# A planner that gives VectorE and GpSimd their shared way to SBUF in turn, and a weight's sign written as a byte by ScalarE

## The chip, the cores and the metric

The kernel runs on one core of a Trainium2 chip. The core has TensorE (PE in the profile, its weight loads PEld), VectorE (DVE), ScalarE (ACT), GpSimd (POOL), and SyncE (SP), which issues the DMAs here. The metric is the device time of one execution in microseconds; the time before is the median of three runs.

## What is computed

Causal attention for 4 batches of 12 heads (448 rows of 64), then a mixing by the real part of a two-dimensional Fourier transform, a layer norm and a feed-forward of 768 to 3072 to 768:

```python
def _moe_ref(x, w_ch1, w_ch2):
    X = np.fft.fft(np.fft.fft(x, axis=1), axis=2)
    u = x + np.real(X).astype(np.float32)
    mu = np.mean(u, axis=-1, keepdims=True)
    var = np.mean((u - mu) ** 2, axis=-1, keepdims=True)
    un = (u - mu) / np.sqrt(var + 1e-06)
    return (u + np.maximum(un @ w_ch1, 0.0) @ w_ch2).astype(np.float32)

def reference(q, k, v, w_ch1, w_ch2):
    x = attention(q, k, v)          # causal softmax, heads side by side: (4, 448, 768)
    return _moe_ref(x, w_ch1, w_ch2)
```

The two weight matrices arrive as 64-bit floating point numbers. They lie in HBM as pairs of 32-bit words, and the kernel itself makes float32 of them.

## The kernel before

**Stages.** Attention runs over 24 pairs of heads (`attend`), six to a batch. After each batch its Fourier transform and norm follow (`fold`, `dft`), mixed among the next pairs. The feed-forward runs over two groups of two batches, and in each over 12 chunks of 256 hidden columns: `f1` makes the hidden values (L978, PSUM tile h), `f2` multiplies them with the second weights (L1219 for group 0, L1180 for group 1, PSUM tile o) and VectorE adds the result into acc (L1168). Every float32 product is made of three passes over a high and a low half (names ending in h and l; w1 and w2h, w2l are such halves of weights). Chunks before `C_FAST` are multiplied in eight blocks of nine matmuls, later ones in seven by Strassen's scheme (`fast`), which needs sums of blocks of weights (ws, L824) and of inputs (us, L930) and adds the running sums c (copied by L335, added to by L1051). Group 1 uses sums in `f2` too (L867, L878, L1108, L1118).

**Conversion of weights.** In group 0 each chunk needs four halves of 128x768 numbers, two of each matrix, 48 in all. Function `weights` (L733 to L780) takes a half w, whose last axis is the low and the high word: ScalarE writes the magnitude of the high word into w32 (L742) and three low bits, taken from one byte, into the low word (L746). VectorE joins the sign bit with these bits (L752), limits and scales the magnitude (L758), and joins the magnitude, shifted by three bits, with the rest (L762). ScalarE then rounds to the high half (L775, or L335 through `copy`), and the low half is the difference (L779 on GpSimd, or L811 on VectorE or GpSimd). The results are kept in HBM (wf, wp), and group 1 reloads them.

**Order.** Every operation is a unit of the class `Plan`, with a cost, a priority, and the tiles it reads and writes. `order()` takes, over and over, the unit that can start first (then by priority) on a list of engines; a unit that may run on several engines goes to the one where start, a bias and SLOW times its cost are least. Each engine then runs its units in that order, and waits by semaphores for data alone. VectorE and GpSimd share a way to SBUF: for units of GpSimd, and those of VectorE that touch no PSUM tile (`side`), `takes` stretches the costs while both run, to a rate of `BOTH`: 0.42 for VectorE, 0.72 for GpSimd. The tables at the top set how many buffers each tile has (`N_W` for w, `N_W32` for w32, `N_QK`, `N_RAW`, `N_PA`) and when units fall due.

Of the kernel before, what the change touches and what calls it, by code (L numbers as in the profile page):

```python
# [51 lines left out]
W_HIGH = float(np.uint32((1151 << 20) - 1).view(np.float32))  # L52
# [23 lines left out]
class Plan:  # L76
# [11 lines left out]
    def add(self, eng, cost, prio, fn, rd=(), wr=(), phase=None):  # L88
# [8 lines left out]
        self.units.append(dict(  # L97
            n=n, engs=dict(zip(eng, cost)) if many else {eng: cost}, many=many, prio=prio, fn=fn, deps=deps, phase=phase,
            new=sorted({z[:2] for z in wr if z[0] in self.bufs}, key=str)))

    def order(self):
# [87 lines left out]

        while len(seq) < len(units):  # L190
            best = None
            for e, cand in pool.items():
                for n in cand:
                    u = units[n]
                    t = when(n, e)
                    if t is None:
# [16 lines left out]
            u["eng"], cost = e, takes(n, e, t)  # L213
            if e in now and side[e][n]:
                x = "G" if e == "V" else "V"
                o = now[x]
                if o is not None and end[o] > t:
                    late = (min(t + cost, end[o]) - t) * (1 - BOTH[x])
                    end[o] += late
                    free[x] += late  # L220
                    for m in succ[o]:
                        for y in units[m]["engs"]:
                            ready[m][y] = max(ready[m][y], end[o] + self.LAT.get((x, y), 100))
            if e in now:
                now[e] = n if side[e][n] else None
# [39 lines left out]
def tile_kernel(ctx, tc, qk, vv, w1, w2, cc, cd, cs, out):  # L265
    nc = tc.nc if tc else None
    T = {}
# [120 lines left out]
    def attend(i):  # L388
# [50 lines left out]
        for k, rows in enumerate(rows_):  # L439
# [82 lines left out]
        for k, (rd, parts) in enumerate((  # L522
                ([(*pa, 0, 0), (*pa, 0, 384), (*pa, 1, 0)], [(0, 0, S, pa, 0, S)]),
                ([(*pg2, 2, 0)], [(1, 128, 256, pg2, 0, 256)]),
                ([(*pg3, 3, 0), (*pa, 1, 384)],
                 [(2, 256, 128, pg3, 0, 128), (1, 384, 64, pg3, 256, 64), (2, 384, 64, pg3, 384, 64), (3, 384, 64, pa, 896, 64)]))):
            def f(parts=parts):
                for c, q0, w, src, s0, sd in parts:
                    kk = min(128, S - 128 * c)
                    for h in range(2):  # L530
# [52 lines left out]
    def dft(b, p0, dp):  # L583
# [6 lines left out]
        for par in range(2):  # L590
# [47 lines left out]
            for sign in range(2):  # L638
# [84 lines left out]
    def weights(j, nm, half, p0):  # L723
# [670 lines left out]
```

## Time and profile before

| what | value |
|---|---|
| median of the runs | 942.95 us (942.83 to 944.33) |
| profiled execution, span | 942.7 us, 16159 instructions |
| TensorE busy | 903.4 us (96%) |
| VectorE busy | 796.9 us (85%) |
| GpSimd busy | 627.6 us (67%) |
| ScalarE busy | 545.3 us (58%) |
| HBM | 112.89 MB read, 54.74 MB written |

TensorE's matmuls are pipelined, so its busy share says that something is in its pipe, not that it runs at its peak. A VectorE or GpSimd instruction counts as busy while it waits for the shared way, so its mean length against its shortest tells of that waiting.

### The profile page before, as it was taken

To read this page: it belongs to the slowest core of one execution; us is meant where nothing else is said; L and a number is where in the kernel's file an instruction comes from. 1 tells how busy PE (TensorE), PEld (TensorE's weight loads), DVE (VectorE), ACT (ScalarE), POOL (GpSimd) and SP (SyncE) were. 2 spreads that over 40 slices of the span, in tenths; PEclk is the share of its full clock that TensorE was granted. 3 is DMA by queue.
4 is the path that set the end of the run, shared out by engine and by line. 5 is a ranking of instruction groups with operands and counts; after the bars stand their busy time and mean duration, and the time that the engine had idled before them with its cause. 6 is when DMAs were issued, how large, how long until landed. Compare 5 with 4: busy or idle time off the path is not lost.

```text
span 942.7 us, 16159 instructions
## 1 busy us (share of the span) xinstructions
PE 903.4 (96%) x5636; PEld 805.8 (85%) x5636; DVE 796.9 (85%) x1330; ACT 545.3 (58%) x1300; POOL 627.6 (67%) x648
## 2 busy tenths in 40 slices
PE   7999999999799999999999988999999999999998
PEld 4667668777688999988989887998999999999998
DVE  6889999898897887999998999997788676666668
ACT  6999798988644444545454456645454453444442
POOL 4798698884642222443543337799999898887886
PEclk9999999999899999999999999999999999999999
DMA  7624624615569556758777668665123444444403
GB/s 274 220 88 170 183 77 138 164 45 180 149 210 345 171 208 224 245 196 292 277 275 256 214 217 295 210 217 174 48 68 118 129 139 136 141 145 136 149 1 117
DMA packets 67537, 165.84 MB, mean 176 GB/s; under 512 B 18976, under 2 KB 31904, under 8 KB 67360
## 3 DMA queue, kind: packets, MB, share of 16 engines
q1 hardware_dynamic: 67456, 164.82, 52.8%
q8 instruction: 44, 0.72, 0.3%
q14 instruction: 37, 0.30, 0.1%
HBM read 112.89 MB, written 54.74 MB: 178 GB/s over the span
## 4 chain that ended last, share of the span: by engine, by line
PE 60%; DVE 21%; POOL 6%; issue 6%; ACT 6%; DMA 1%; SPq 0%; POOLq 0%; DVEq 0%; ACTq 0%
PE h L978 22%; PE o L1180 16%; PE o L1219 8%; PE x L531 4%; PE pt L505 3%; PE sc L457 3%; DVE acc L1168 3%; DVE w L762 3%; DVE w L752 2%; ACT p L473 2%; DVE w L811 1%; DVE w L758 1%; DVE mn L469 1%; DVE ws L824 1%; DVE hl L1015 1%
## 5 line engine op out<-in xcount | busy, mean ns | idle before, releaser
L1168 DVE TENSOR_TENSOR acc<-o,acc 128x384 f32<-128x384 f32 x444 | 236.8, 552 | 79.9 <-PE o L1180 56.3
L1219 PE MATMUL o<-w2l,hh 128*128 128x384 f32 x336 | 113.6, 338 | 1.4 <-POOL w2l L779 1.3
L1219 PE MATMUL o<-w2h,hh 128*128 128x384 f32 x336 | 113.3, 337 | 1.6 <-DVE acc L1168 1.6
L1219 PE MATMUL o<-w2h,hl 128*128 128x384 f32 x336 | 113.1, 337 | 0.0
L779 POOL TENSOR_TENSOR w2l<-w,w2h 128x768 fp32r<-128x768 f32 x24 | 49.7, 2071 | 78.6 <-ACT w2h L775 71.6
L494 POOL TENSOR_TENSOR p<-p,ri 128x128 f32<-128x128 f32 (+3 forms) x113 | 79.1, 729 | 22.0 <-DVE ri L485 18.1
L811 POOL TENSOR_TENSOR w<-w,w 128x384 fp32r<-128x384 f32 x33 | 39.7, 1203 | 60.1 <-ACT w L335 59.1
L978 PE MATMUL h<-u11h,w 128*128 128x448 f32 x174 | 64.8, 380 | 3.4 <-ACT u11h L335 3.0
L1219 PEld LDWEIGHTS o<-w2l,hh 128*128 128x128 f32 x336 | 63.1, 188 | 4.4 <-POOL w2l L779 2.6
L1219 PEld LDWEIGHTS o<-w2h,hh 128*128 128x128 f32 x336 | 63.2, 188 | 4.2 <-DVE acc L1168 2.3
L978 PE MATMUL h<-u22h,w 128*128 128x448 f32 x174 | 63.2, 371 | 3.2 <-DVE c L1051 3.2
L1180 PE MATMUL o<-w2h,hh 128*128 128x384 f32 x288 | 65.1, 339 | 0.3 <-DVE acc L1168 0.3
L978 PE MATMUL h<-u12h,w 128*128 128x448 f32 x174 | 64.1, 370 | 0.0
L1219 PEld LDWEIGHTS o<-w2h,hl 128*128 128x128 f32 x336 | 63.2, 188 | 0.0
L978 PE MATMUL h<-u21h,w 128*128 128x448 f32 x174 | 63.0, 367 | 0.0
L1180 PE MATMUL o<-w2l,hl 128*128 128x384 f32 x288 | 62.4, 338 | 0.4 <-DVE acc L1168 0.4
L505 PE MATMUL pt<-cst,p 128*128 128x128 f32 (+1 forms) x384 | 56.9, 281 | 2.6 <-ACT p L492 1.9
L505 PEld LDWEIGHTS pt<-cst,p 128*128 128x128 f32 (+1 forms) x384 | 41.4, 139 | 16.8 <-issue 5.7
L335 ACT COPY c<-h 128x448 f32<-128x448 f32 x57 | 30.1, 529 | 44.1 <-PE h L978 40.2
L867 POOL TENSOR_TENSOR w2h<-w,w2h 128x384 fp32r<-128x384 f32 x43 | 45.8, 1065 | 14.6 <-ACT w2h L335 14.6
L473 ACT ACTIVATE p<-sc,mn 128x448 f32<-128x448 f32 (+3 forms) x96 | 50.4, 525 | 7.6 <-DVE mn L469 6.7
L1180 PEld LDWEIGHTS o<-w2h,hh 128*128 128x128 f32 x288 | 52.1, 188 | 2.6 <-DVE acc L1168 0.6
(212 smaller groups left out, 2999.7 us busy)
## 6 DMA issues: line engine op xcount, KB each, us to landing
w<-in_w_dram SPq DMA_DIRECT2D x48, 768.0 KB, 4.9
wp<-w SPq DMA_DIRECT2D x49, 384.0 KB, 3.5
w<-wp SPq DMA_DIRECT2D x49, 384.0 KB, 3.1
wf<-w SPq DMA_DIRECT2D x34, 384.0 KB, 2.9
w<-wf SPq DMA_DIRECT2D x17, 768.0 KB, 4.3
raw<-in_qk_dram SPq DMA_DIRECT2D x23, 480.0 KB, 3.8
us<-und SPq DMA_DIRECT2D x45, 224.0 KB, 4.2
v<-in_vv_dram SPq DMA_DIRECT2D x24, 256.0 KB, 2.9
```

The lines of the kernel that those rows point to most:

```text
L335: nc.scalar.copy(out=out, in_=in_)
L473: nc.scalar.activation(out=T[pb][:, PO[rr]:PO[rr] + n], in_=T[ps][:, c0:c0 + n], func=ACTF.Exp, scale=-1.0, bias=T[mn][:, rr:rr + 1], accu ...
L494: nc.gpsimd.tensor_tensor(out=x, in0=x, in1=z.to_broadcast([128, KE[r]]), op=ALU.mult)
L505: nc.tensor.transpose(T[ps][0:m, 128 * k:128 * k + 128], T[pb][:, PO[r] + 128 * c:PO[r] + 128 * c + m], T["cst", 0][:, 0:128])
L531: nc.tensor.matmul(out=T[xps][64 * h:64 * h + 64, q0:q0 + w], lhsT=T[v][0:kk, c, h * D:(h + 1) * D], rhs=T[src][0:kk, s0 + h * sd:s0 + h * ...
L779: nc.gpsimd.tensor_tensor(out=T[wl], in0=T[w32].bitcast(F32), in1=T[wh], op=ALU.subtract)
L811: (nc.gpsimd if eng == "G" else nc.vector).tensor_tensor(out=T[z][:, 1], in0=src(), in1=T[z][:, 0], op=ALU.subtract)
L867: (nc.gpsimd if eng == "G" else nc.vector).tensor_tensor(out=T[z][:, 384:768], in0=src(), in1=T[z][:, 0:384], op=ALU.subtract)
L978: nc.tensor.matmul(out=T[ps][:, 0:S], lhsT=a[:, t], rhs=x[:, t], start=start and k == 0, stop=stop and k == 8, skip_group_check=True)
L1168: nc.vector.tensor_tensor(out=x, in0=T[ps][:, 0:384], in1=x, op=ALU.add)
L1180: nc.tensor.matmul(out=T[ps][:, 0:384], lhsT=hpart(j, h, a)[:, k * 128:k * 128 + 128], rhs=T[z][:, 384 * b:384 * b + 384], start=start and ...
L1219: nc.tensor.matmul(out=T[ps][:, 0:384], lhsT=T[a][:, m, k * 128:(k + 1) * 128], rhs=w[:, sl], start=(m == 0 and z == 0), stop=(m == 1 and ...
```

## The change

Four things change together.

1. The planner no longer stretches costs. A unit that uses the shared way starts, in the plan, no earlier than 91 ns (VectorE) or 42 ns (GpSimd) before the other engine's last such unit ends (`OVER`). Units given `port=False` (reciprocal, bn_stats, bn_aggr) don't count as users.
2. In `weights`, ScalarE writes the sign as a byte into the top of the low word, by Prelu with a slope of 2^100 for negative numbers, over the three bits' word. VectorE's L752 goes; its last join reads the low word. The scaling moves from VectorE's L758 into ScalarE's L742.
3. Buffers and due times: three w and w32 where there were two, four of each q and k half for three, three raw for two, four c for three, one pa for two; the DMA scratch area of GpSimd shrinks to 1024 bytes. `C_FAST` goes from 5 to 4, `C_MIX` from 7 to 5, and many due times move.
4. Some costs in the tables.

```diff
-N_RAW, N_V, N_QK, N_PT, N_W, N_W32, N_PA = 2, 2, 3, 2, 2, 2, 2
+N_RAW, N_V, N_QK, N_PT, N_W, N_W32, N_PA = 3, 2, 4, 2, 3, 3, 1
-SPLIT_AT, FOLD_AT = -509, 5113
+SPLIT_AT, FOLD_AT = -688, 5956
...
-W_LEAD, F2_LAG = 809, 561
+W_LEAD, F2_LAG = 1065, 508
...
-C_FROM, W_FROM, N_WARM = 0, 8, 11
-N_W1, N_C, N_WS, C_FAST, C_MIX = 7, 3, 3, 5, 7
+C_FROM, W_FROM, N_WARM = 3, 8, 11
+N_W1, N_C, N_WS, C_FAST, C_MIX = 7, 4, 3, 4, 5
...
-BOTH = dict(V=0.42, G=0.72)
-SLOW, BIAS = 1.5, dict(S=-300, V=-100, G=-500)
+OVER = dict(V=91, G=42)
+SLOW, BIAS = 1.843, dict(S=-300, V=-100, G=-427)
...
-        def takes(n, e, t):
-            c = units[n]["engs"][e]
-            o = now.get("G" if e == "V" else "V") if e in now and side[e][n] else None
-            if o is None or end[o] <= t:
-                return c
-            both = end[o] - t
-            return c / BOTH[e] if c <= both * BOTH[e] else c + both * (1 - BOTH[e])
+        held = {"V": 0.0, "G": 0.0}
 
         def when(n, e):
             s = slot(units[n], e)
-            return None if s is None else max(free[e], ready[n][e], s)
+            if s is None:
+                return None
+            t = max(free[e], ready[n][e], s)
+            if e in held and side[e][n]:
+                t = max(t, held["G" if e == "V" else "V"] - OVER[e])
+            return t
...
         def f():
-            nc.scalar.activation(out=T[w32].bitcast(F32), in_=T[w][:, :, 1].bitcast(F32), func=ACTF.Abs)
+            nc.scalar.activation(out=T[w32].bitcast(F32), in_=T[w][:, :, 1].bitcast(F32), func=ACTF.Abs, scale=W_SCALE)
...
         def f():
-            x = T[w][:, :, 1]
+            nc.scalar.activation(
+                out=T[w].bitcast(I8)[:, :, 3], in_=T[w][:, :, 1].bitcast(F32), func=ACTF.Prelu, scale=SIGN_SCALE, alpha=SIGN_ALPHA)
+        add("S", acts(768) + 75, p0 + 1, f, rd=[w, (*w, 1)], wr=[(*w, 2)], phase="W")
+
+        def f():
+            x = T[w32].bitcast(F32)
+            nc.vector.tensor_scalar(out=x, in0=x, scalar1=W_TOP, scalar2=None, op0=ALU.min)
+        add("V", dve(768, 1.92) + 4, p0 + 2, f, rd=[(*w32, 0)], wr=[(*w32, 1)], phase="W")
+
+        def f():
             nc.vector.scalar_tensor_tensor(
-                out=x, in0=x, scalar=0x80000000, in1=T[w][:, :, 0], op0=ALU.bitwise_and, op1=ALU.bitwise_or)
...
-                out=T[w32], in0=T[w32], scalar=3, in1=T[w][:, :, 1], op0=ALU.logical_shift_left, op1=ALU.bitwise_or)
+                out=T[w32], in0=T[w32], scalar=3, in1=T[w][:, :, 0], op0=ALU.logical_shift_left, op1=ALU.bitwise_or)
```

What the change makes of the order is shown at three places. In the kernel after, lines stand some twelve lower: L731, L735 and L740 are ScalarE's passes over a half (L740 the sign), L746 and L750 VectorE's limit and join, L767 the low half on GpSimd, L799 the low halves of w1, L812 the sums ws, L1156 the additions into acc, L918 the sums us, L324 copies and casts, L997 the hidden values, L763 the high half. w_ with a number is a buffer of w1 or w32.

VectorE, one fast chunk late in group 0, before:

```order
L758 TENSOR_SCALAR w_6861<-w_6861 128x768
L1168 TENSOR_TENSOR acc_4497<-o_6864,acc_4497 128x384
L752 SCALAR_TENSOR_TENSOR w<-w 128x768
L1168 TENSOR_TENSOR acc_4497<-o_6875,acc_4497 128x384
L762 SCALAR_TENSOR_TENSOR w_6861<-w_6861,w 128x768
L1168 TENSOR_TENSOR acc_4502<-o_6891,acc_4502 128x384
L824 TENSOR_TENSOR ws<-ws,w_6819 128x384
L811 TENSOR_TENSOR w_6933<-ws,w_6933 128x384
```

and a fast chunk of the kernel after, about as late:

```order
L750 SCALAR_TENSOR_TENSOR w_6766<-w_6766,w 128x768
L812 TENSOR_TENSOR ws<-w_6766 128x384
L1156 TENSOR_TENSOR acc_4532<-o_6804,acc_4532 128x384
L812 TENSOR_TENSOR ws<-ws,w_6696 128x384
L812 TENSOR_TENSOR ws<-w_6696,w_6766 128x384
L1156 TENSOR_TENSOR acc_4534<-o_6820,acc_4534 128x384
L799 TENSOR_TENSOR w_6831<-ws,w_6831 128x384
L799 TENSOR_TENSOR w_6837<-ws,w_6837 128x384
L799 TENSOR_TENSOR w_6847<-ws,w_6847 128x384
L812 TENSOR_TENSOR ws<-w_6696,ws 128x384
```

The join before L762 is gone, and all four sums ws of a chunk stand on VectorE, where one stood.

GpSimd, the same chunks, before:

```order
L811 TENSOR_TENSOR w_6856<-w_6819,w_6856 128x384
L811 TENSOR_TENSOR w_6883<-w_6819,w_6883 128x384
L824 TENSOR_TENSOR ws<-w_6861 128x384
L824 TENSOR_TENSOR ws<-w_6819,w_6861 128x384
L824 TENSOR_TENSOR ws<-w_6819,ws 128x384
L811 TENSOR_TENSOR w_6971<-ws,w_6971 128x384
L779 TENSOR_TENSOR w2l<-w_6963,w2h 128x768
L779 TENSOR_TENSOR w2l<-w_6982,w2h 128x768
```

and after, where between the first row and the last nothing but L767 stands:

```order
L918 TENSOR_TENSOR us<-us 128x448
L767 TENSOR_TENSOR w2l<-w_5514,w2h 128x768
L767 TENSOR_TENSOR w2l<-w_5635,w2h 128x768
L767 TENSOR_TENSOR w2l<-w_5748,w2h 128x768
L767 TENSOR_TENSOR w2l<-w_5977,w2h 128x768
```

Fourteen more rows of L767 follow that differ in the buffer alone. Counted over the whole program, GpSimd has 11 L811 for 58 (2 for 37 ahead of group 1), 6 L824 for 26 (none for 21), 2 L905 for 25, 4 L930 for 11, 31 L867 for 85, 24 L1118 for 38 and 97 L494 for 113; VectorE has most of what these lose; the 16 L494 go to ScalarE.

ScalarE, the conversions of that chunk with the copy of c behind them, before:

```order
L742 ACTIVATE w_6388<-w 128x768
L742 ACTIVATE w_6415<-w 128x768
L746 ACTIVATE w<-w 128x768
L775 CAST w2h<-w_6388 128x768
L1009 ACTIVATE hh<-c 128x448
L335 COPY c<-h 128x448 x2
```

and after:

```order
L731 ACTIVATE w_6562<-w 128x768
L735 ACTIVATE w<-w 128x768
L324 COPY c<-h 128x448
L740 ACTIVATE w<-w 128x768
L997 ACTIVATE hh<-c 128x448
L731 ACTIVATE w_6601<-w 128x768
L763 CAST w2h<-w_6562 128x768
```

Each half has a third pass, L740, among the copies of c and the casts. No load of a function table is added: there is one in the program, before and after.

## Rows read from the trace of the kernel before

**Rows 1.** Busy us by stretch: PE, PEld, DVE, ACT, POOL (count), clock, DMA, GB/s.

```profile
20.00:243.00 223.00, 212.98 (x1940) 156.75 (x1940) 197.32 (x400) 199.42 (x612) 179.10 (x226) 1.00 0.46 141
243.00:300.00 57.00, 52.42 (x306) 48.55 (x307) 51.92 (x76) 27.80 (x51) 28.35 (x27) 0.94 0.73 235
300.00:390.00 90.00, 90.00 (x480) 86.01 (x479) 73.14 (x113) 43.60 (x66) 24.02 (x17) 1.00 0.62 216
390.00:640.00 250.00, 234.91 (x1234) 220.38 (x1232) 236.90 (x335) 128.09 (x222) 130.83 (x95) 1.00 0.71 247
640.00:760.00 120.00, 118.95 (x617) 112.01 (x618) 96.05 (x156) 60.40 (x139) 113.50 (x112) 0.99 0.31 102
```

**Rows 2.** Waits of TensorE in 390 to 640: us in all, times, longest.

```profile
PE h L978 <- ACT c L335: 9.3, 7, 2.8
PE h L978 <- DVE c L1051: 3.2, 3, 1.7
```

**Rows 3.** VectorE's groups in 390 to 640: count, busy us, mean ns, idle before.

```profile
L1168 DVE TENSOR_TENSOR acc<-o,acc 128x384 f32<-128x384 f32 x119 | 61.8, 547 | 5.4 <-PE o L1219 5.3
L762 DVE SCALAR_TENSOR_TENSOR w<-w,w 128x768 uint32<-128x768 uint32 x27 | 32.1, 1189 | 0.0
L752 DVE SCALAR_TENSOR_TENSOR w<-w 128x768 uint32<-128x768 uint32 x26 | 28.9, 1111 | 0.7 <-ACT w L742 0.5 <-ACT w L746 0.2
L1015 DVE SCALAR_TENSOR_TENSOR hl<-c,hh 128x448 fp32r<-128x448 f32 x21 | 19.3, 918 | 2.4 <-ACT hh L1009 2.3
L811 DVE TENSOR_TENSOR w<-ws,w 128x384 fp32r<-128x384 f32 x20 | 16.8, 869 | 0.9 <-ACT w L335 0.9
```

**Rows 4.** Timeline of 420 to 432: start, length (us), instruction.

```profile
421.33 0.96 DVE L752 SCALAR_TENSOR_TENSOR w<-w 128x768 uint32<-128x768 uint32 x1 [0.49 <-ACT w L742]
...
421.77 1.39 POOL L811 TENSOR_TENSOR w<-ws,w 128x384 fp32r<-128x384 f32 x1 [1.92 <-ACT w L335]
...
422.20 1.37 DVE L758 TENSOR_SCALAR w<-w 128x768 f32<-128x768 f32 x1
...
430.07 0.54 DVE L811 TENSOR_TENSOR w<-ws,w 128x384 fp32r<-128x384 f32 x1
...
430.54 0.61 DVE L1015 SCALAR_TENSOR_TENSOR hl<-h,hh 128x448 fp32r<-128x448 f32 x1
...
431.07 0.61 DVE L1015 SCALAR_TENSOR_TENSOR hl<-c,hh 128x448 fp32r<-128x448 f32 x1
```

**Rows 5.** ScalarE's groups in 390 to 640, as rows 3.

```profile
L746 ACT ACTIVATE w<-w 128x768 uint32<-128x768 uint8 x26 | 23.7, 913 | 7.3 <-DMA w<-in_w_dram 7.3
...
L335 ACT COPY c<-h 128x448 f32<-128x448 f32 x25 | 13.1, 527 | 8.0 <-PE h L978 7.3 <-POOL us L1118 0.4
```

**Rows 6.** GpSimd's groups in 390 to 640, as rows 3.

```profile
L779 POOL TENSOR_TENSOR w2l<-w,w2h 128x768 fp32r<-128x768 f32 x15 | 33.1, 2204 | 36.1 <-ACT w2h L775 36.1
L811 POOL TENSOR_TENSOR w<-w,w 128x384 fp32r<-128x384 f32 x15 | 18.7, 1244 | 35.1 <-ACT w L335 35.1
```

**Rows 7.** The chain that ended last, one piece: start, us, what, instructions.

```profile
306.56 3.71 PE h L978 x18
```

**Rows 8.** The same chain where the feed-forward starts.

```profile
242.95 1.59 DVE u11l L905
```

**Rows 9.** Busy time and clock of 240 to 250, as rows 1.

```profile
240.00:250.00 10.00, 5.89 (x16) 5.07 (x17) 9.68 (x10) 6.38 (x13) 9.31 (x8) 0.68 0.42 115
```

**Rows 10.** Groups of three engines in attention, 20 to 243, as rows 3.

```profile
L494 POOL TENSOR_TENSOR p<-p,ri 128x128 f32<-128x128 f32 (+3 forms) x105 | 74.6, 739 | 19.7 <-DVE ri L485 15.8 <-PE sd L457 2.4 <-ACT xt L335 1.1
...
L427 DVE SCALAR_TENSOR_TENSOR ql<-raw,qh 128x512 fp32r<-128x512 f32 x21 | 19.4, 925 | 0.7 <-ACT qh L421 0.7
...
L337 DVE COPY pa<-pt 128x128 f32<-128x128 f32 (+2 forms) x14 | 5.3, 381 | 6.6 <-ACT pa L335 5.5 <-PE pt L505 1.0
```

**Rows 11.** VectorE's timeline in the first pair, as rows 4.

```profile
11.40 0.69 DVE L427 SCALAR_TENSOR_TENSOR ql<-raw,qh 128x512 fp32r<-128x512 f32 x1
```

More of the change, by code (lines that the diff above doesn't have):

```diff
@@ L14 @@
 U8 = mybir.dt.uint8
+I8 = mybir.dt.int8
 ACTF = mybir.ActivationFunctionType
@@ L39 @@
 AFTER = dict(E1=("A1",), E2=("A1", "A2"), L=("Q",))
-C_FROM, W_FROM, N_WARM = 0, 8, 11
-N_W1, N_C, N_WS, C_FAST, C_MIX = 7, 3, 3, 5, 7
-MIX_LEAD, FILL_LEAD = -94, 417
-LATER = dict(S=-1500, V=-248, G=-847)
+C_FROM, W_FROM, N_WARM = 3, 8, 11
+N_W1, N_C, N_WS, C_FAST, C_MIX = 7, 4, 3, 4, 5
+MIX_LEAD, FILL_LEAD = 270, 472
+LATER = dict(S=-1401, V=-399, G=-847)
 F0 = 1e6
 AGAIN = dict(S=-1500, V=-100, G=-1000)
-NORM_AT, TR_AT = 1675, 1894
+NORM_AT, TR_AT = 1675, 1763
 N_UB, N_US = 3, 5
-BOTH = dict(V=0.42, G=0.72)
-SLOW, BIAS = 1.5, dict(S=-300, V=-100, G=-500)
+OVER = dict(V=91, G=42)
+SLOW, BIAS = 1.843, dict(S=-300, V=-100, G=-427)
 BIG = float(2 ** 30)
 W_SCALE = 2.0 ** -112
-W_HIGH = float(np.uint32((1151 << 20) - 1).view(np.float32))
+W_TOP = float(np.uint32((1151 << 20) - 1).view(np.float32)) * W_SCALE
+SIGN_SCALE, SIGN_ALPHA = 2.0 ** -20, 2.0 ** 100
 ORDER = (
@@ L86, in __init__, with add @@
         self.units, self.writers, self.uses = [], {}, {}
-    def add(self, eng, cost, prio, fn, rd=(), wr=(), phase=None):
+    def add(self, eng, cost, prio, fn, rd=(), wr=(), phase=None, port=True):
         n = len(self.units)
@@ L97, in add @@
         self.units.append(dict(
-            n=n, engs=dict(zip(eng, cost)) if many else {eng: cost}, many=many, prio=prio, fn=fn, deps=deps, phase=phase,
+            n=n, engs=dict(zip(eng, cost)) if many else {eng: cost}, many=many, prio=prio, fn=fn, deps=deps, phase=phase, port=port,
             new=sorted({z[:2] for z in wr if z[0] in self.bufs}, key=str)))
@@ L173, in order @@
         side = {
-            e: [e == "G" or e == "V" and not any(key[0] in self.banks for key in tiles_of[u["n"]]) for u in units]
+            e: [e == "G" or e == "V" and u["port"] and not any(key[0] in self.banks for key in tiles_of[u["n"]]) for u in units]
             for e in "VG"}
-        now = {"V": None, "G": None}
-        def takes(n, e, t):
-            c = units[n]["engs"][e]
-            o = now.get("G" if e == "V" else "V") if e in now and side[e][n] else None
-            if o is None or end[o] <= t:
-                return c
-            both = end[o] - t
-            return c / BOTH[e] if c <= both * BOTH[e] else c + both * (1 - BOTH[e])
+        held = {"V": 0.0, "G": 0.0}
         def when(n, e):
             s = slot(units[n], e)
-            return None if s is None else max(free[e], ready[n][e], s)
+            if s is None:
[4 more added lines that the diff above has]
+            return t
         while len(seq) < len(units):
@@ L199, in order @@
                         bias = BIAS if u["phase"] in "AQ" else LATER if u["prio"] < F0 + 1000 * (NCH - 1) else AGAIN
-                        mine = t + bias[e] + takes(n, e, t) * SLOW
-                        if any(s + bias[x] + takes(n, x, s) * SLOW < mine for x, s in (
+                        mine = t + bias[e] + u["engs"][e] * SLOW
+                        if any(s is not None and s + bias[x] + u["engs"][x] * SLOW < mine for x, s in (
                                 (x, when(n, x)) for x in u["engs"] if x != e)):
@@ L212, in order @@
                 pool[x].remove(n)
[L213 to L225, printed above, removed]
+            u["eng"], cost = e, u["engs"][e]
             free[e] = t + cost
+            if e in held and side[e][n]:
+                held[e] = free[e]
             fin = free[e]
@@ L460, in attend @@
             n = sum(KE[r] for r in rows)
-            add("PE", 3 * mm(n) * 1.086 + (60 if tail else 110 * len(rows) + 200), p0, f, rd=[qh, ql, kh, kl, ("idb", 0), ("mkb", 0)], wr=banks, phase="A")
+            add("PE", 3 * mm(n) * 1.086 + (65 if tail else 165 * len(rows) + 195), p0, f, rd=[qh, ql, kh, kl, ("idb", 0), ("mkb", 0)], wr=banks, phase="A")
             for y, r in enumerate(rows):
@@ L533, in f @@
                             rhs=T[src][0:kk, s0 + h * sd:s0 + h * sd + w], start=c == 0, stop=c == 3)
-            add("PE", mm(sum(z[2] for z in parts), 4) + 21 * len(parts) + 105 * (k == 2), base + TR_AT + 700 + 250 * k, f,
+            add("PE", mm(sum(z[2] for z in parts), 4) + 21 * len(parts) + (95, 100, 175)[k], base + TR_AT + 700 + 250 * k, f,
                 rd=[v, *rd, *([(*xps, k - 1)] if k else [])], wr=[(*xps, k)], phase="A")
```

15 lines of the change are left out of this document (6 added, 9 removed).

## The prediction, before the run

> **What bounds the kernel now.** I read the busy time by stretch first [rows 1]. The run has three stages: attention and Fourier transforms (20 to 243 us), the first half of the feed-forward, in which the weights are converted on the fly (243 to 640), and its second half, which reloads them converted. The reader is to see that TensorE is busy 90.00 of 90 us in 300 to 390: there nothing else matters. In 390 to 640 it stands 250 - 234.91 = 15.1 us, and VectorE is busy 236.90 of 250, with ScalarE at 128 and GpSimd at 131. In attention all four are high: TensorE 213 of 223, ScalarE 199, VectorE 197, GpSimd 179.
>
> Then the waits of TensorE in 390 to 640 [rows 2]: most of the named time is for the running sums c (9.3 us for ScalarE's copy, 3.2 for VectorE's addition). The copy itself is short; what comes ahead of it in the in-order engines is the conversion. So I read VectorE's groups there [rows 3]: 119 additions into acc at 547 ns, which read PSUM; and next to them groups that work in SBUF alone and whose means are far over their undisturbed times. The timeline shows why [rows 4]: GpSimd's L811 holds from 421.77 for 1.39 us, to 423.16; VectorE's L758 starts at 422.20, is out at 423.57, 0.41 behind GpSimd's end. The L811 of 430.07, with no GpSimd instruction beside it, takes 0.54 against a mean of 869 ns. So much of VectorE's "busy" is standing in a queue for the way that it shares with GpSimd.
>
> The Trainium skill (SBUF — State Buffer, section "A bandwidth-pool intuition that's wrong") says that this pair of ports is a lock: who comes second waits to the end, nothing is shared. The planner of before slows both engines instead (its BOTH, 0.42 and 0.72). By the shared rate, an instruction of 1.2 us taken off GpSimd would give VectorE back at most 1.2 x (1 - 0.42) = 0.7 us; by the lock, up to all 1.2. The 0.41 above fits the lock, and no sum below needs the page.
>
> **The change, part by part.** *The join L752 goes.* 48 of them leave VectorE; 26 lie in 390 to 640, 28.9 us of its busy time there [rows 3]. In 300 to 390 the same removal is worth nothing, since TensorE hides it.
>
> *Its replacement* is one more pass of 768 on ScalarE for each of the 48 halves. The nearest row is L746, same count and same stride of 8 bytes, 913 ns [rows 5]: 26 x 0.913 = 23.7 us onto 128 of 250. Bounds: 0.5 us each (the 527 ns copy of 448) to 1.8 (two of L746), so 13 to 47 us; I take L746. ScalarE stays under 70% busy; the cover is the deeper buffers (three w and w32 where there were two), and what queues behind it is the copy of c.
>
> *The plan moves work from GpSimd to VectorE.* By the order, ahead of group 1 there leave GpSimd 35 of 37 L811, 21 of 21 L824, 23 of 25 L905 and 7 of 11 L930: 86. What stays is its 24 L779 and little else. Some 70 of the 86 lie in 390 to 640, with a few more that the extra fast chunk adds: 74 onto VectorE, by the distance between starts 0.47 us for 384 columns and 0.53 for 448 [rows 4]: 48 x 0.47 + 26 x 0.53 = 36.3 us.
>
> *Stalls that go.* The four groups L762, L752, L1015 and L811 of [rows 3] against 0.96, 0.96, 0.61 and 0.54 undisturbed [rows 4]: 27 x 0.23 + 26 x 0.15 + 21 x 0.31 + 20 x 0.33 = 6.2 + 3.9 + 6.5 + 6.6 = 23.2 us in 97.1 us of busy time. Of the other 236.9 - 97.1 - 61.8 (acc) = 78 us, at the same quarter where it works in SBUF, another 16: 39 in all, 35 without L752's own. What remains is caused by 15 L779, 33.1 us of GpSimd [rows 6]: at worst 28 us of stalls, at best 5; I take 18, since an addition from PSUM of half a microsecond fits beside each.
>
> VectorE in 390 to 640: 236.9 - 28.9 - 35 + 36.3 + 18 = 227 us (217 to 237). If the stretch keeps its ratio to VectorE's time, 250 x 227 / 236.9 = 239.6, a gain of 10; if TensorE's own 234.9 becomes the end, 15.1. I take **-12**.
>
> *The fifth chunk is multiplied in seven products for eight* (C_FAST 4): 9 matmuls fewer; 18 take 3.71 us [rows 7], so **-1.9**, on a stretch that TensorE bounds.
>
> *The passage at 243 us.* TensorE waits for u11l, 1.59 us on VectorE [rows 8], against 0.53 undisturbed, and after this standing its granted clock is 0.68 in 240 to 250, that is partly at 1.2 GHz, with 5.89 of 10 busy [rows 9]. 243 to 300 has 57 - 52.42 = 4.6 us of standing and 57 x 0.06 = 3.4 lost to the clock [rows 1]. The low halves of u move to VectorE alone; the reload and ScalarE's share of the chain stay. Of these 8 us I take **-2.5** (0 to -5).
>
> *Group 1.* 54 of the 85 L867 and 14 L1118 leave GpSimd, which is 113.5 of 120 busy in 640 to 760 with VectorE at 96 [rows 1]. TensorE stands 1.05 there and has 1.2 of clock to regain: **-1.5**.
>
> *Attention.* 22 SBUF operations come from GpSimd at about 0.6 and 31 copies and casts from ScalarE at about 0.4 (L337, [rows 10]): 13.2 + 12.4 = 25.6 us onto VectorE's 197 of 223. GpSimd loses those 22 and 16 of its L494 at 0.74; VectorE's stalls fall with that: L427 alone has 21 x (0.925 - 0.69) = 4.9 us of them [rows 10, 11]. With all its groups I hold 7 to 18 us back. That leaves 205 to 216 of 223, so I take **0**: from -6 (part of the 10 us that TensorE stands) to +25.6 (nothing given back, all of it late). The second pa buffer goes too; pair i+1 copies into pa only when pair i's x is through, which the order already spaces.
>
> Sum: -12 - 1.9 - 2.5 - 1.5 + 0 = -17.9. The profiled span, 942.7, is 0.25 us from the median of the runs, 942.95, so nothing is to be added: **925.0**.
>
> **The rivals.** *More comes back:* 390 to 640 at TensorE's own 234.9 (-15.1), attention -6, the passage -4.6, group 1 -2.5, matmuls -1.9: -30, so 913. For it: GpSimd nearly empties. Against: VectorE still carries 227 of 235.
>
> *ScalarE stands in front:* 25 copies of c in 390 to 640 share an in-order queue with 26 new passes; if TensorE waits half a pass, 0.46 us, for each, 11.5 of the 12 go: 936.5. For it: [rows 2] names this very copy. Against: ScalarE idles half of that stretch. Attention that costs 8 to 12 us more comes out at the same place, 933 to 937.
>
> *Slower, attention ends on VectorE:* its 25.6 us all arrive at the end because the stalls don't fall, 942.95 - 17.9 + 25.6 = 950.7. It is slower than before once over 19.8 of the 25.6 arrive. For it: VectorE at 88% and four engines in step; against: GpSimd loses 16 x 0.74 and 22 at twice VectorE's 0.6, some 38 of its 179 us there.
>
> *It doesn't do what it says:* VectorE and GpSimd run in their own order on the chip and no instruction waits for the other's turn; if they meet as often as before, stalls stay at 28 in 390 to 640, VectorE is at 237 and only -1.9 - 2.5 - 1.5 and little else remain: 937, with the case before.
>
> **How the numbers follow.** The forecast, 918 to 932, has 0.46. More comes back (906 to 917): 0.18. Half of it lost to ScalarE, to attention or to stalls that stay (933 to 941): 0.20. No change that can be told, 941.1 to 944.8: 0.05. Slower: 0.11. I count 0.2% (1.9 us) as the least that a measurement of this kernel tells. Faster is 0.46 + 0.18 + 0.20 = 0.84. The range 908 to 941 leaves out 0.16 above and about 0.03 below.
>
> **What would show it.** Right: in the stretch that was 390 to 640, TensorE at 97% or more, VectorE's L762 and L811 within 10% of 0.96 and 0.54, GpSimd under 25% busy. Attention still ends by 240 to 246. Wrong: an L905 of u11l over 8 us later than the 242.95 of [rows 8] (attention), waits of TensorE for ScalarE's c above 9.3 us (the queue), or L746's successor far from 0.91.

## The result, and the profile after

The kernel after takes **917.76 us** (median, 916.33 to 918.28) beside 943.64 us (942.83 to 945.46) for the kernel before on the same chip: ratio **0.9714**, 95% interval 0.9687 to 0.9740. The prediction was 925.0 us, 908 to 941, and faster at 0.84. So the sign and the range were right and the forecast was 7 us short: 917.76 lies at the edge between the forecast (918 to 932) and the rival *more comes back* (906 to 917). The experiments below show that a good part of the reason given was not right.

The profiled execution of after spans 916.5 us, 26.2 less than that of before. Busy time by stretch, columns as in [rows 1]; the stretches are the stages of the new kernel:

```profile
20.00:244.00 224.00, 214.37 (x1945) 160.14 (x1943) 201.84 (x452) 205.73 (x605) 131.58 (x189) 0.98 0.50 158
244.00:300.00 56.00, 55.08 (x316) 50.95 (x317) 44.34 (x76) 35.84 (x57) 18.20 (x19) 0.94 0.74 239
300.00:384.00 84.00, 84.00 (x457) 80.97 (x456) 70.15 (x126) 66.52 (x78) 13.00 (x7) 1.00 0.70 240
384.00:622.00 238.00, 236.67 (x1256) 225.68 (x1255) 204.53 (x368) 172.25 (x254) 56.08 (x39) 1.00 0.76 263
622.00:740.00 118.00, 118.00 (x633) 114.01 (x632) 99.13 (x177) 56.90 (x133) 83.27 (x86) 1.00 0.38 124
```

In 384 to 622, which answers to 390 to 640 of before, TensorE is busy 236.67 of 238 us (99.4%), where it stood 15.1 us [rows 1]. VectorE has gone from 95% to 86% and GpSimd from 52% to 24%; ScalarE has risen from 51% to 72%. 244 to 300 has 0.92 us of standing where there were 4.6, with the same mean clock, 0.94.

The same can be read off the chain of work that ended last. This is its share by line inside group 0 (the view cuts the row off), of before in 293 to 645:

```profile
by line: PE o L1219 22.3%; PE h L978 18.7%; issue 9.4%; DVE w L762 6.3%; DVE acc L1168 6.1%; DVE w L752 5.5%; DVE w L758 3.3%; DVE w L811 3.2%; DVE ws L824 3.0%; DVE hl L1015 2.6%; DVE c L1051 2.3%; POOL w L811 2.1%; POOL ws L824 1.8%; DVE 
```

and of after in 299 to 621:

```profile
by line: PE o L1207 49.9%; PE h L966 39.1%; issue 1.4%; DVE w L799 1.3%; DVE ws L812 1.2%; ACT w L740 1.2%; DVE w L750 1.0%; DVE acc L1156 0.9%; DVE hl L1003 0.7%; DVE us L918 0.7%; ACT w L324 0.6%; DVE w L746 0.4%; ACT c L324 0.3%; ACT w2h
```

TensorE's two lines make 41% of the chain before and 89% after: group 0 has come to TensorE's own pace. Its waits in 244 to 622 (us in all, times, longest), where [rows 2] had 9.3 and 3.2 for c:

```profile
PE h L966 <- ACT u11h L324: 3.1, 1, 3.1
PE h L966 <- ACT c L324: 1.2, 2, 0.7
```

VectorE's groups in 384 to 622, columns as in [rows 3]:

```profile
L1156 DVE TENSOR_TENSOR acc<-o,acc 128x384 f32<-128x384 f32 x117 | 62.2, 549 | 13.6 <-PE o L1207 13.5
L750 DVE SCALAR_TENSOR_TENSOR w<-w,w 128x768 uint32<-128x768 uint32 x27 | 25.7, 955 | 12.2 <-ACT w L740 12.1
L799 DVE TENSOR_TENSOR w<-ws,w 128x384 fp32r<-128x384 f32 x37 | 19.9, 555 | 2.0 <-ACT w L324 1.9
L799 DVE TENSOR_TENSOR w<-w,w 128x384 fp32r<-128x384 f32 x26 | 16.9, 658 | 2.9 <-ACT w L324 2.7
...
L1003 DVE SCALAR_TENSOR_TENSOR hl<-c,hh 128x448 fp32r<-128x448 f32 x23 | 14.9, 651 | 0.0
```

The second join takes 955 ns where it took 1189, the low halves of sums 555 where they took 869, hl from c 651 where it took 918 [rows 3]; the addition into acc, which touches PSUM, was 547 and is 549. New is the idle time ahead of L750: VectorE now stands 12.1 us for ScalarE's sign. That pass is not what the prediction took it for. ScalarE's groups of the whole run:

```profile
L740 ACT ACTIVATE w<-w 128x768 int8<-128x768 f32 x48 | 94.0, 1959 | 0.7
L735 ACT ACTIVATE w<-w 128x768 uint32<-128x768 uint8 x48 | 43.8, 913 | 2.8 <-DMA w<-in_w_dram 2.8
```

### The profile page after: what moved, and what is told of

It reads as the page before. It is cut to its first block, busy times and chain, and to the rows that moved or that the text cites. A ratio compares the mean times of both kernels' runs of the same rounds, so it can differ in the third digit from the quotient of the medians.

```text
span 916.5 us, 16107 instructions
## 1 busy us (share of the span) xinstructions
PE 898.0 (98%) x5627; PEld 809.8 (88%) x5627; DVE 774.7 (85%) x1493; ACT 620.5 (68%) x1331; POOL 397.3 (43%) x452
## 4 chain that ended last, share of the span: by engine, by line
PE 82%; ACT 7%; DVE 7%; issue 1%; POOL 1%; DMA 1%; SPq 0%; ACTq 0%; DVEq 0%
PE h L966 32%; PE o L1207 18%; PE o L1168 17%; PE sc L446 4%; PE x L520 4%; PE pt L494 4%; ACT p L462 2%; PE ay L590 2%; ACT w L740 1%; DVE mn L458 1%; PE at L684 1%; DMA raw<-in_qk_dram 1%; DVE w L750 1%; PE sc L438 1%; ACT p L481 1%
## 5 line engine op out<-in xcount | busy, mean ns | idle before, releaser
L1156 DVE TENSOR_TENSOR acc<-o,acc 128x384 f32<-128x384 f32 x444 | 237.4, 550 | 53.9 <-PE o L1168 35.3
L767 POOL TENSOR_TENSOR w2l<-w,w2h 128x768 fp32r<-128x768 f32 x24 | 46.0, 1918 | 241.8 <-ACT w2h L763 203.2
L740 ACT ACTIVATE w<-w 128x768 int8<-128x768 f32 x48 | 94.0, 1959 | 0.7
L483 POOL TENSOR_TENSOR p<-p,ri 128x128 f32<-128x128 f32 (+2 forms) x97 | 58.2, 625 | 52.9 <-DVE ri L474 25.1
L324 ACT COPY c<-h 128x448 f32<-128x448 f32 x59 | 31.3, 531 | 63.0 <-PE h L966 62.9
L966 PE MATMUL h<-u11h,w 128*128 128x448 f32 x168 | 62.7, 380 | 3.1 <-ACT u11h L324 3.1
L1168 PE MATMUL o<-w2l,hl 128*128 128x384 f32 x288 | 64.6, 338 | 0.0
L750 DVE SCALAR_TENSOR_TENSOR w<-w,w 128x768 uint32<-128x768 uint32 x48 | 46.7, 976 | 17.8 <-ACT w L740 17.7
L966 PE MATMUL h<-u12h,w 128*128 128x448 f32 x168 | 61.5, 367 | 0.0
L494 PE MATMUL pt<-cst,p 128*128 128x128 f32 (+1 forms) x384 | 57.4, 286 | 0.8 <-ACT bs L324 0.7
L494 PEld LDWEIGHTS pt<-cst,p 128*128 128x128 f32 (+1 forms) x384 | 44.3, 144 | 12.3 <-issue 5.9
```

Of the source, the lines that this page charges most:

```text
L483: nc.gpsimd.tensor_tensor(out=x, in0=x, in1=z.to_broadcast([128, KE[r]]), op=ALU.mult)
L494: nc.tensor.transpose(T[ps][0:m, 128 * k:128 * k + 128], T[pb][:, PO[r] + 128 * c:PO[r] + 128 * c + m], T["cst", 0][:, 0:128])
L740: nc.scalar.activation(out=T[w].bitcast(I8)[:, :, 3], in_=T[w][:, :, 1].bitcast(F32), func=ACTF.Prelu, scale=SIGN_SCALE, alpha=SIGN_ALPHA)
L750: nc.vector.scalar_tensor_tensor(out=T[w32], in0=T[w32], scalar=3, in1=T[w][:, :, 0], op0=ALU.logical_shift_left, op1=ALU.bitwise_or)
L767: nc.gpsimd.tensor_tensor(out=T[wl], in0=T[w32].bitcast(F32), in1=T[wh], op=ALU.subtract)
L966: nc.tensor.matmul(out=T[ps][:, 0:S], lhsT=a[:, t], rhs=x[:, t], start=start and k == 0, stop=stop and k == 8, skip_group_check=True)
```

## The experiments

The change was taken apart into its sign pass, its turns and its buffers. Each kernel is planned anew from its edit, so the order moves with it. The measure that turned out to tell them apart is **group 0 in full**, from the first matmul of `f1` to the last of `f2` of that group, and how long TensorE stands in it. Two such rows, of before:

```profile
241.50:645.30 403.80, 383.10 (x2037) 360.00 (x2038) 365.34 (x525) 202.97 (x344) 188.18 (x143) 0.99 0.69 237
```

and of after:

```profile
244.40:621.30 376.90, 375.05 (x2022) 356.93 (x2023) 318.68 (x567) 273.51 (x385) 86.18 (x65) 0.99 0.74 254
```

All kernels by such rows (standing is length less TensorE's busy time; buffers are those of w and w32; "old" or "new" are the due times, `C_FAST`, the other buffers and the costs; each row of group 0 is one profiled execution):

| kernel | sign by | planner | w, w32 | dates | ratio to before | starts at | group 0 | TensorE stands | VectorE | ScalarE | GpSimd |
|---|---|---|---|---|---|---|---|---|---|---|---|
| before | VectorE | stretch | 2, 2 | old | 1 | 241.5 | 403.8 | 20.7 | 365 | 203 | 188 |
| b_sign | ScalarE | stretch | 2, 2 | old | 1.0106 | 246.6 | 411.5 | 23.2 | 332 | 277 | 170 |
| b_turns | VectorE | turns | 2, 2 | old | 0.9917 | 243.7 | 392.6 | 13.7 | 341 | 200 | 122 |
| b_sign_turns | ScalarE | turns | 2, 2 | old | 0.9969 | 242.7 | 401.7 | 18.4 | 317 | 282 | 113 |
| a_w2 | ScalarE | turns | 2, 2 | new | 0.9977 | 237.9 | 407.4 | 22.6 | 331 | 282 | 83 |
| a_w_only2 | ScalarE | turns | 2, 3 | new | 0.9897 | 240.2 | 403.0 | 18.3 | 323 | 275 | 85 |
| a_w32_only2 | ScalarE | turns | 3, 2 | new | 0.9797 | 241.5 | 388.0 | 10.3 | 323 | 274 | 85 |
| a_no_turns | ScalarE | stretch | 3, 3 | new | 0.9886 | 242.0 | 395.1 | 16.4 | 335 | 273 | 153 |
| b_turns_w3 | VectorE | turns | 3, 3 | old | 0.9830 | 258.8 | 373.1 | 2.8 | 333 | 194 | 124 |
| a_no_sign | VectorE | turns | 3, 3 | new | 0.9726 | 239.2 | 381.0 | 6.0 | 348 | 199 | 86 |
| after | ScalarE | turns | 3, 3 | new | 0.9714 | 244.4 | 376.9 | 1.9 | 319 | 274 | 86 |
| a_i16 | ScalarE, two slow passes | turns | 3, 3 | new | 1.0015 | 245.9 | 404.5 | 21.5 | 321 | 314 | 85 |

### The two halves of the change on the kernel before

*The sign by ScalarE alone* (b_sign; the scaling moves with it, as in the change):

```diff
...
-                out=x, in0=x, scalar=0x80000000, in1=T[w][:, :, 0], op0=ALU.bitwise_and, op1=ALU.bitwise_or)
+                out=T[w].bitcast(I8)[:, :, 3], in_=T[w][:, :, 1].bitcast(F32), func=ACTF.Prelu, scale=SIGN_SCALE, alpha=SIGN_ALPHA)
```

> The kernel before with the sign written by ScalarE, and nothing else changed: the planner that stretches costs, its buffers and due times stay. The whole change measured 0.9714 of before, some 26 us. Theory 1 (the turns empty GpSimd, and VectorE's standing for the shared way goes): most of the stalls stay, since GpSimd keeps 104 units of group 0 where it had 118; -3 to -9 us, so 934 to 940. Theory 2 (the join's 52 us on VectorE are what counts): -18 to -26, so 917 to 925. Theory 3 (deeper buffers and due times let the conversion run ahead): -2 to -6. The sign pass itself: 1.96 us each, as in the kernel after.

Measured: 957.4 us, ratio 1.0106 (1.0066 to 1.0147): 1% longer, where all three theories had it shorter. VectorE loses 33 us of work in group 0 and TensorE stands longer all the same, above all for c and for the low halves of w2 (waits of the whole run):

```profile
PE h L980 <- ACT c L338: 13.2, 10, 4.4
PE o L1221 <- POOL w2l L781: 4.9, 4, 1.5
```

So the removal of the join is no gain by itself. This kernel lacks the deeper buffers that the prediction named as the cover of the new pass; with them, a_no_sign below tests the same term.

*The turns alone* (b_turns), the planner's part of the diff, `OVER`, `SLOW`, `BIAS` and `port`:

```diff
-BOTH = dict(V=0.42, G=0.72)
-SLOW, BIAS = 1.5, dict(S=-300, V=-100, G=-500)
+OVER = dict(V=91, G=42)
+SLOW, BIAS = 1.843, dict(S=-300, V=-100, G=-427)
```

> The kernel before with the planner that gives the way in turn (its 91 and 42 ns, SLOW, BIAS, and the units that count as no users), while the join L752 stays on VectorE and the buffers and due times are those of before. GpSimd has 69 units of group 0 for 118. Theory 1: -12 to -20, so 923 to 931. Theory 2: within 5 us of before, since VectorE has 46 units more in group 0 and none less. Theory 3: within 5 us.

Measured: 937.99 us, 0.9917 (0.9889 to 0.9944). A real gain of 8 us: GpSimd's 188 us in group 0 fall to 122, and VectorE, which takes that work over, is busy 24.5 us *less* than before.

*Both, with the old buffers and dates* (b_sign_turns; the two edits above together):

> Both together with the buffers, due times and C_FAST of before. Theories 1 and 2 both: -20 to -25, so 918 to 923, the rest being the 9 matmuls and the start. Theory 3: at most half of the gain, -6 to -13.

Measured: 942.39 us, 0.9969 (0.9947 to 0.9992). The sign takes back more than half of what the turns gave. What makes the 26 us of the whole change is in neither of them nor in the two together.

### What the kernel after owes to each

*After with the old planner* (a_no_turns; the lines of b_turns the other way):

> The kernel after with the planner of before, that stretches costs by 0.42 and 0.72 (SLOW and BIAS as before too); sign, buffers, due times and C_FAST as after. GpSimd gets 86 units of group 0 for the 32 of after. Theory 1: half or more of the gain is lost, 930 to 940. Theory 2: it stays at 917 to 923. Theory 3: 917 to 925. Due times were set for the other planner, which may cost some us in attention under any theory; the stretch of group 0 tells them apart: by theory 1 TensorE stands there again by 8 us or more.

Measured: 935.09 us, 0.9886 (0.9857 to 0.9915), 0.0172 above after's ratio, some 16 us; in group 0 TensorE stands 16.4 us where after has 1.9. The turns are worth about twice as much here as on the kernel before. Whether by the turns themselves or by the work that they move isn't told apart: the planner decides both at once, and no run held the one and changed the other.

*After with VectorE's join* (a_no_sign; the lines of b_sign the other way):

> The kernel after with the conversion of before: the join L752 is back on VectorE, ScalarE's pass L740 is gone; planner, buffers, due times and C_FAST as after. Before with the sign alone came out at 1.0106, so the sign may cost rather than bring. Theory 2 (VectorE's load counts): VectorE gets 45 units more in group 0 than after, TensorE stands again there: 928 to 938. Theory 3 with the turns (the deeper buffers and the emptied GpSimd do it, the sign is not needed): within 4 us of after, 914 to 921.

Measured: 919.78 us, 0.9726 (0.9689 to 0.9764): within the interval of after. In group 0 VectorE is busy 348 of 381.0 us, 29.5 more than in after, and TensorE stands only 6.0. So a VectorE at 91% holds TensorE up very little, once the rest is in place.

*After with Copy for Prelu* (a_copy). No sign is written, so the weights come out positive; order and instructions are otherwise those of after. It was to show whether the length of L740 comes from the function:

```diff
-... func=ACTF.Prelu, scale=SIGN_SCALE, alpha=SIGN_ALPHA)
+... func=ACTF.Copy, scale=SIGN_SCALE)
```

> The kernel after with the same order of instructions, the third pass by the plain Copy function for Prelu; this writes no sign, so all weights come out positive, and the text says so. It measures the disputed cost: if the byte output or the stride makes 1.96 us, the pass stays at 1.9 to 2.0; if the function does, it falls to 0.9. Where ScalarE's 48 us more are hidden by the deep buffers: within 2 us of after, 916 to 920. Where they are what is left of standing: 911 to 915.

Measured: 916.5 us, 0.9682 (0.9649 to 0.9715). The pass is as long as before, in ScalarE's groups:

```profile
L740 ACT ACTIVATE w<-w 128x768 int8<-128x768 f32 x48 | 94.1, 1961 | 0.7
```

So it isn't the function. Beside a_no_sign on the same chip, 3.3 us lower in the medians and 5.3 us in group 0 (375.7 for 381.0), the run also bounds what the sign pass is worth in the end: a few microseconds, with intervals that overlap. *The same edit on b_sign* (b_sign_copy, also without the sign) was to make its pass shorter:

> The kernel of b_sign (before, with the sign pass by ScalarE) with Copy for Prelu, same order; weights come out positive. If the loss of b_sign, 10 us and a TensorE wait of 13.2 us for ScalarE's c, comes from the length of the pass, 1.96 for 0.91 us, this one is 10 to 20 us faster than b_sign, 932 to 942, faster than before, as theory 2 says of VectorE. If it comes from one more link in the chain whatever its length, it stays within 5 us of b_sign's 1.0106.

Measured: 957.36 us, 1.0108 (1.0065 to 1.0150), the time of b_sign, since its pass is no shorter. So it can't tell whether b_sign loses by the length of the new link or by its being there; that stays open.

### The third buffers

*After with two buffers of w and of w32* (a_w2):

```diff
-N_RAW, N_V, N_QK, N_PT, N_W, N_W32, N_PA = 3, 2, 4, 2, 3, 3, 1
+N_RAW, N_V, N_QK, N_PT, N_W, N_W32, N_PA = 3, 2, 4, 2, 2, 2, 1
```

> The kernel after with two buffers of w and of w32 for three, all else as after; the plan gives GpSimd 33 units of group 0, as after (32). Theory 3 in its narrow form (it is these buffers that let the longer chain of the conversion run ahead): 8 to 20 us lost, 926 to 938, and TensorE waits for ScalarE's c again. If other parts (C_FAST, due times, the turns) do it: within 4 us of after.

Measured: 943.78 us, 0.9977 (0.9960 to 0.9995). Nearly the whole gain is gone, more than the 8 to 20 us expected, with GpSimd as empty as in after (83 us for 86) and VectorE 34 us below before. The waits for c are back (whole run):

```profile
PE h L966 <- ACT c L324: 14.3, 8, 4.4
```

The chain that ended last shows what c is behind. Its share by line in 300 to 645 (the view cuts the row off):

```profile
by line: PE o L1207 19.0%; PE h L966 17.3%; ACT w L740 5.9%; issue 4.2%; DVE w L750 3.4%; DVE w L799 3.4%; ACT w L731 2.9%; DVE acc L1156 2.9%; DVE ws L812 2.6%; ACT w L735 2.6%; ACT w L324 2.2%; DMA us<-td 1.6%; ACT w2h L763 1.4%; ACT c L3
```

TensorE's two lines make 36% where after has 89%, and ScalarE's three passes and VectorE's join 15%. One piece of the chain (start, us, what; pieces named "issue", of 0.02 us but for one of 0.37 at the cut, are left out):

```profile
445.10 0.81 ACT w L735
445.93 1.96 ACT w L740
447.92 0.97 DVE w L750
...
449.33 0.51 ACT w L324
449.85 0.80 ACT w L731
450.65 0.83 ACT w L735
451.50 1.97 ACT w L740
453.50 0.96 DVE w L750
```

ScalarE's three passes over a half, VectorE's join and the casts of the joined half (L324) follow each other link by link, one half every 5.6 us (445.93 to 451.50), and TensorE isn't in this piece at all. Even all 48 halves at this pace would be 269 us, in a group of 407, so the round decides in pieces and not all along. The join closes the round in two ways. In ScalarE's in-order queue the cast of the joined half stands ahead of the next L731; its row in the timeline of a_w2 has the wait for the join:

```profile
448.92 0.93 ACT L324 CAST w<-w 128x384 fp32r<-128x384 f32 x2 [0.65 <-DVE w L750]
```

And SyncE's load of a later w waits for the join, since it needs the buffer: in the waits of its queue, 72.1 us in 16 in a_w2,

```profile
SPq L727 <- DVE w L750: 72.1, 16, 11.7
```

and 41.6 in after:

```profile
SPq L727 <- DVE w L750: 41.6, 14, 7.8
```

This sum doesn't say how much of TensorE's standing comes by this second way: it is 68.3 us in a_w32_only2, which stands 10.3, and 47.1 in a_i16, which stands 21.5:

```profile
SPq L727 <- DVE w L750: 68.3, 14, 11.5
SPq L729 <- DVE w L752: 47.1, 14, 6.6
```

How the copy gets into it is in ScalarE's timeline of a_w2:

```profile
497.09 0.89 ACT L731 ACTIVATE w<-w 128x768 f32<-128x768 f32 x1
497.88 0.89 ACT L735 ACTIVATE w<-w 128x768 uint32<-128x768 uint8 x1
498.80 1.90 ACT L740 ACTIVATE w<-w 128x768 int8<-128x768 f32 x1
500.45 0.62 ACT L324 COPY c<-h 128x448 f32<-128x448 f32 x1
```

The copy stands behind three passes that began at 497.09. The first matmul after it is in TensorE's timeline:

```profile
501.13 0.50 PE L966 MATMUL h<-t4h,w 128*128 128x448 f32 x1 [2.80 <-ACT c L324]
```

TensorE has waited 2.80 us for that copy. This is the prediction's rival *ScalarE stands in front*, and it is real where buffers are two.

*Two of w alone* (a_w_only2, `N_W, N_W32` = 2, 3):

> The kernel after with two buffers of w (the loaded 64-bit half) and three of w32. Two buffers of both gave 0.9977 where after gave 0.9714. If it is the load that comes too late, since it waits until the last join has read w: most of that loss is back here, 0.990 to 1.000. If w32, which is held until the last low half is made, is the narrow one: within 0.4% of after, 0.968 to 0.976.

Measured: 936.72 us (933.35 to 940.39; the profile in the table is of the longest), 0.9897 (0.9876 to 0.9919). Here the load itself is a link of the chain, right behind the join that frees its buffer:

```profile
569.67 0.97 DVE w L750
...
570.66 4.61 DMA w<-in_w_dram
```

*Two of w32 alone* (a_w32_only2, 3, 2):

> The kernel after with three buffers of w and two of w32. The counterpart of the run with two w: if the late load is the cause, 0.968 to 0.978; if w32 is the narrow one, 0.988 to 1.000. Should both runs lose over 1%, a half needs both at once and either is enough to stop the chain.

Measured: 926.17 us, 0.9797 (0.9782 to 0.9811). Either buffer alone gives part; the third w is the larger part. The prices overlap: 0.0263 for the two buffers and 0.0172 for the planner make more than the 0.0286 of the whole, so each is worth most where the other is in place.

*The kernel before with the turns and three of each, join kept* (b_turns_w3; the scratch area has to shrink for them):

```diff
-N_RAW, N_V, N_QK, N_PT, N_W, N_W32, N_PA = 2, 2, 3, 2, 2, 2, 2
+N_RAW, N_V, N_QK, N_PT, N_W, N_W32, N_PA = 2, 2, 3, 2, 3, 3, 2
```

> The kernel before with the turns and three buffers of w and w32 (and the scratch area of 1024 bytes that makes room), with the join on VectorE, the due times, C_FAST and the other buffers of before. If turns and these buffers are what the change consists of: 0.970 to 0.980 (the 9 matmuls, 0.002, are missing). If the due times or C_FAST carry a part: 0.982 to 0.990, little under the 0.9917 of the turns alone.

Measured: 929.45 us, 0.9830 (0.9816 to 0.9845), against b_turns at 0.9917. TensorE stands 2.8 us in group 0, where b_turns has 13.7. But attention ends at 258.8 us, 15 us later, with one long wait for VectorE:

```profile
PE ay L588 <- DVE fh L324: 7.4, 1, 7.4
```

The later start also gives the conversion a lead, so its 373.1 us aren't to be set against the 376.9 of after. With buffers and turns, but neither the sign nor the dates, six tenths of the gain are there (0.0170 of 0.0286); a_no_sign, which has the dates as well, has nearly all.

### What makes the sign pass slow, and how near ScalarE is

*Both words' passes into 16 bits* (a_i16): the three bits go into the low 16 bits of the word, the sign into the high 16.

```diff
-                out=T[w][:, :, 0], in_=T[w].bitcast(U8)[:, :, 3], func=ACTF.Copy, ...
+                out=T[w].bitcast(U16)[:, :, 0], in_=T[w].bitcast(U8)[:, :, 3], func=ACTF.Copy, ...
-                out=T[w].bitcast(I8)[:, :, 3], in_=...
+                out=T[w].bitcast(I16)[:, :, 1], in_=...
```

> The kernel after, same order, with the low word of a half written as two 16-bit halves: the three bits as an unsigned 16-bit number, the sign as a signed one, for the byte. It measures the price by output width: if only one-byte output is slow, both passes take 0.9 us, and ScalarE is 50 us less busy; if every output under four bytes costs double, both take 1.9 to 2.0 and ScalarE has 48 us more. For the time: with 0.9 within 0.4% of after (the plan had 0.81 in it), 0.967 to 0.974; with 1.96 for both, 0.975 to 0.990, since ScalarE then has 230 of 250 us where group 0 is bound by TensorE.

Measured: 947.22 us, 1.0015 (1.0003 to 1.0027), beyond the 0.975 to 0.990 expected for two slow passes. The pass over the bits, 913 ns into a 32-bit word, now takes as long as the sign's:

```profile
L737 ACT ACTIVATE w<-w 128x768 uint16<-128x768 uint8 x48 | 93.9, 1956 | 1.5 <-DMA w<-in_w_dram 1.5
L742 ACT ACTIVATE w<-w 128x768 int16<-128x768 f32 x48 | 93.5, 1949 | 0.7
```

So the output's width does it: 16 bits cost what 8 do. And 41 us more on ScalarE in group 0 (314 for 274) bring back 19.7 us of standing, with 9.6 us of waits for c. So the kernel after works just short of the point where ScalarE's passes decide, and ScalarE's 72% isn't the slack that it looks like. Whether they decide by ScalarE's load or by the longer way of each half isn't told apart.

## Why the prediction was right, and where it was not

**Right in size, nearly.** In the profiles, before to after: the end of attention moves by +2.9 us (241.5 to 244.4), group 0 in full by -26.9, the rest (group 1) by -2.2; together -26.2. The prediction had 0, -16.4 (its -12, -1.9 and -2.5) and -1.5. TensorE's standing in group 0 falls by 18.9 us (20.7 to 1.9); there are 15 matmuls fewer in the stretch by the records, some 3 us at the pace of [rows 7], nine of them those of `C_FAST`; about 5 us more are time in which TensorE counts as busy with the same work, and I can't put them down to a line. At most 1.5 of them are clock: in before the granted clock is 0.50, that is 1.2 GHz, from 639.5 to 642.9 us, with TensorE busy 3.06 of these 3.4, and after has no such stretch in group 0 behind 251.2 (1.00). The passage at 243 us gave 3.7 of standing where I took 2.5. So the feed-forward went as the rival *more comes back* had it (15.1 + 4.6 + 1.9 + 2.5 = 24.1), and its hope for attention, -6, did not come.

**Attention** was taken as 0 and came to +2.9 here; in a_copy, which has the same order, it ended at 240.7, so a few microseconds of it vary from one execution to the next. VectorE is busy 201.84 of 224 there, not the 205 to 216 that I had counted, and GpSimd 131.58. The rival that attention ends on VectorE did not happen.

**The step that failed first: "Its replacement", 0.913 us from the nearest row.** L740 took 1,959 ns, outside my bounds of 0.5 to 1.8. The row that I took, L746, agrees in count and stride but writes 32 bits, and that was the difference that mattered. 24 of them made 47.0 us in 384 to 622, where I had 26 and 23.7, and ScalarE was busy 72% and not under 70. My list had named this as a sign that I was wrong ("far from 0.91"), and it was; the total held only because of the next step.

**The step that failed in its weight: "the cover is the deeper buffers".** The prediction named the third buffers as what hides ScalarE's pass and didn't price their absence. With two buffers the sign costs 9.1 us of group 0 (b_turns 392.6, b_sign_turns 401.7) and 0.0052 of the ratio; with three it gives 4 us of group 0 (a_no_sign 381.0, after 376.9), with ratios that can't be told apart. Taken out of after, the third buffers take back 0.0263 of the 0.0286.

**The rule that failed: "If the stretch keeps its ratio to VectorE's time".** I bounded the stretch by VectorE's load, 237 to 227 us. VectorE fell to 204.53 in 384 to 622, so I also overstated what stays; of the 18 us of stalls that I left in, the groups shown hold about 5, against the undisturbed lengths of [rows 4]: 26 x (0.658 - 0.54) and 37 x (0.555 - 0.54) of L799, 23 x (0.651 - 0.61) of L1003. But the load wasn't the bound. a_w2 has 34 us less on VectorE than before and a group 0 that is 3.6 us longer; a_no_sign has 17 us less than before and one that is 22.8 shorter. That the -12 came out near the measured gain was luck: in its sum the join's removal is what makes VectorE's time fall. Without it, and with L752's own stalls among the 39 that go, the same sum gives 236.9 - 39 + 36.3 + 18 = 252 us, more than before, so the rule would have called that kernel slower; a_no_sign is that kernel, and its ratio is 0.9726. By the chain of a_w2 and the runs on buffers, what held TensorE was the conversion's round through ScalarE and VectorE, which two buffers leave little room to overlap; the next load is shown as a link of it at one place of a_w_only2, where it took 4.61 us, and what it costs in all isn't shown. The busy share of an engine in such a round says how much it works, not how long the round is.

**What held.** By the list of what would show it: TensorE 99.4% (97 or more); GpSimd 23.6% (under 25); L762's successor 955 ns and, for the sums, L811's 555 (within 10% of 0.96 and 0.54), though L811's other form, 658, is outside; attention's end at 244.4 (240 to 246); waits for c 1.2 us (under 9.3). "It doesn't do what it says" fell: in b_turns VectorE takes work over and is less busy for it, and the turns gain in both settings.

**Open.** Whether b_sign loses by the length of its pass; what the turns give beside the work they move; which of the due times, the fourth q and k and the other buffers keep attention short (they were not tried one by one).

## What to carry to other kernels

Where several in-order engines pass one buffer round, follow that round in the chain of waits, link by link, before pricing any engine's load: a longer link can cost 9 us with two buffers and nothing that can be told with three, and one that looks like the bound by its busy share may hold nobody up. Where an edit names a cover, give the cover's own price: here it was worth nine tenths of the gain. And when an operation is new, the nearest row must agree in the width that it writes, not only in size and stride.

## What the runs showed of the hardware

ScalarE's pass over 128x768 numbers, written with a stride of 8 bytes, took 912 to 914 ns into 32-bit words (from bytes; after, b_sign and a_copy) and 1,949 to 1,961 ns into 8 or 16 bits. The function made no difference (Prelu 1,959, Copy 1,961, both into 8 bits), nor did the input (a byte 1,956, a float32 1,949, both into 16 bits, in a_i16). The pass into w32, 32-bit words without a stride, took 906 to 914. Narrow outputs without a stride were not run.

TensorE's standing cost more than itself. In a_w2 it stands 20.7 us longer than in after over the same matmuls, and is busy 9.8 us longer too; this is its group 0:

```profile
237.90:645.30 407.40, 384.85 (x2021) 361.79 (x2022) 330.87 (x572) 281.65 (x388) 82.55 (x63) 0.97 0.69 239
```

384.85 us for 2021 matmuls, where after has 375.05 for 2022; the mean granted clock is 0.97 for 0.99, and 0.02 of 407 us is 8 us of those 9.8. One place where it falls is right behind the wait of 2.80 us shown for a_w2:

```profile
495.00:501.10 6.10, 3.33 (x17) 2.71 (x15) 3.29 (x5) 5.17 (x6) 1.84 (x1) 1.00 0.65 223
501.40:504.90 3.50, 3.50 (x11) 3.09 (x11) 2.66 (x3) 1.31 (x2) 1.82 (x1) 0.51 0.69 223
```

TensorE is busy 3.33 of 6.10 us at a granted clock of 1.00 (2.4 GHz), and the 3.50 us that follow show 0.51, the lower level of 1.2 GHz for nearly all of them.
